# Global indices loaded first, a second column group for the global rows' values, fewer mask products, tile 0 in three pieces, and a new instruction order

## The chip, the cores and the metric

The kernel runs on one core of a Trainium2 chip (trn2). The metric is the device time of one execution in microseconds (us); lower is better.

## The reference

An attention with a window and a few global positions, followed by a two-layer network. Batch 8, 8 heads, 576 positions, 64 numbers a head, 8 global positions.

```python
scores = scale * np.matmul(q, k.transpose(0, 1, 3, 2))
mask = np.abs(pos[:, None] - pos[None, :]) <= 32
mask = mask | is_global[:, None] | is_global[None, :]
scores = np.where(mask, scores, -1e9)          # then softmax along the last axis
x = np.matmul(attn, v)                         # to (4608, 512): heads side by side
h = x @ w_in                                   # (4608, 2048)
g = np.maximum(h, 0.0) + np.log1p(np.exp(-np.abs(h)))   # softplus
out = g @ w_out                                # (4608, 512), float32
```

Only a band of the scores, the 8 global columns and the 8 global rows are computed.

## The kernel before

**The work's units.** Positions are cut into blocks of 32; a *pair* `n` is 4 blocks (128 tokens) of all 8 heads, so there are 36 pairs, 4.5 to a batch. Four pairs make a *tile* `m` of 512 tokens for the network; there are 9. A batch's keys and queries come in on SP's queue (L363, L413), are rounded to bf16 (`cast`, tiles `kb` and `qb`), and are turned (`turn`, L716 and L720) into `kx` and `qx`; its values become `vb`. There is one staging tile for each of q, k and v, so a batch's load can start when the batch before it has been rounded.

**A pair.** TensorE forms the scores `s` (L951). Pairs in `PARTED` (0 to 8) are masked on TensorE: two products of the mask with the identity (L935, L945) are put into the scores' banks first, VectorE takes the maxima (L966), and ACT takes eight exponentials with sums (L983). Other pairs are masked on VectorE: two adds (L955), the maxima (L968), a subtraction on GpSimd (L974), one exponential on ACT (L987), and the sums on VectorE (L994). GpSimd or VectorE divides (`pn`, L1002), VectorE transposes (`pt`, L1011), TensorE forms the values (`xo`, L1110), and ACT and VectorE copy them to `xT`.

**A batch's global rows.** The global queries against all keys (`sg`, L859), maxima (L869), exponentials (`pg`, L876), the transpose `pgt` (L881, L883), and the product with the values, `ov` (L892): 18 key blocks, four products of 32x32 weights and 129 columns each, all key blocks into the same place of one PSUM bank. `gv` (L897, L898) divides and gives `vg`, which `xo` needs.

**The network.** First layer `h` (L1140): 16 column blocks `c`, four products each; softplus on ACT (L1146) to `g`; second layer `o` (L1151): 16 products for each 128 tokens; ACT copies to `osb` and GpSimd or ACT stores. `HALVED = 2` lets tiles 0 and 1 go in two halves of 256 tokens.

**The order** is not written down. Each piece of work is a job with engines, planned costs, dependences, PSUM or buffer needs (`KINDS`, `SLOTS`: of the 8 banks `h` may hold 3) and a rank; `_Order.run` (L185) takes the job that can start first by its planned times, and each engine gets its instructions in that order and runs them strictly so. `stall` plans for TensorE's instruction fetch. `DRAWS` holds 39 random seeds that shift ranks and hold jobs back (`stir`). ACT's exponentials of the next tile are gated by the last softplus of the tile before (`gate`), and the rounding of batch b's keys and queries by the tenth softplus of tile b - 2.

Of the kernel before, what the change touches and what calls it, by code (L numbers as in the profile page):

```python
# [19 lines left out]
class _Order:  # L20
# [260 lines left out]
def kernel(  # L281
# [16 lines left out]
    P = 128  # L298
# [28 lines left out]
    PARTED = range(9)  # L327
    PIECES = 2
    HALVED = 2
    WARM = 34000  # L330
    DRAWS = (3335,3199,2819,96436,96805,4649,6481,3986,84270,10262,19837,43780,47955,95447,65550,91158,57715,12543,70958,16076,24438,75659,29538,93811,54424,2760,89415,85671,84841,4779,10200,27915,85360,19476,26792,78533,69364,53916,4150,)
# [253 lines left out]
    KINDS = dict(h=(3, 0), o=(2, 0), o0=(4, 0), s=(4, 0), tr=(3, 0), pick=(2, 0), sg=(4, 0), ov=(1, 0), xo=(4, 0))  # L585
# [94 lines left out]
    def add_cast(b, w):  # L680
# [6 lines left out]
        for h in range(2):  # L687
            def emit(e, h=h):
                if w == 2:
                    copy(e, vb[b % 2][:, :, h * D:(h + 1) * D], stage[2][:, h, :, :])  # L690
                else:
                    c = slice(h * 2 * NC, (h + 1) * 2 * NC)
                    (scaled, copy)[w](e, (qb, kb)[w][:, c, :, :].rearrange("p c d e -> p c e d"), stage[w][:, c, :, :])
            n = NJ * D
            cost = {"POOL": (1410, 1490), "ACT": (1380, 1480)}
            if b == 1:
                cost["DVE"] = (1290, 1370)
            if b == 0:
                cost = {"POOL": (1150, 1250), "DVE": (880, 960)}
            T["cast", b, w].append(o.add(cost, emit, [T["load", b, w]] + early + gate, rank=10 * phase_of(b) + 4 if b else 1.5 if w == 2 else 0))  # L700

    def add_prep(b):
# [97 lines left out]
        if early:  # L800
# [6 lines left out]
            for w, t in FIRST:  # L807
                for e in range(2 if t < FULL else 1):
# [6 lines left out]
                    T["last", w] = T["tr", b, w, t, e] = o.add({"PE": (330, 500) if b else (880, 1050) if t == 0 else (480, 650)}, lambda eng, w=w, t=t, e=e: tr(w, t, e),  # L815
# [18 lines left out]
        T["fill", b] = o.add({"DVE": (410, 490), "ACT": (470, 570)}, fill, [T["put", b, 1]] + blanked, rank=rank - 1 if b else 0, uses=[kkey])  # L834
# [11 lines left out]
    def add_global(b, gate):  # L846
# [39 lines left out]
        def ov(e, m0, m1):  # L886
            if m0 == 0:
                PS["ov", b] = psum(("ov", b), [P, 2 * D + 1], FP32)
            ps = PS["ov", b]
            for m in range(m0, m1):  # L890
                for c in range(R):
                    nc.tensor.matmul(out=ps[quad(c), :], lhsT=pgt[quad(c), m, 0:2 * NG, :].rearrange("p g h -> p (g h)"),  # L892
                                     rhs=vb[i][quad(c), m, 0:2 * D + 1], start=(m == 0), stop=(m == NJ - 1))
# [10 lines left out]
        heads = ((0, 1),) if b else ((0,), (1,))  # L904
        mxs, exps, tps, ovs = [], [], [], []
        for hs in heads:
            mxs.append(o.add({"DVE": (1680, 1760) if b else (860, 940)}, lambda e, hs=hs: mx(e, hs), [T["sg", b]], rank=rank, uses=keys, behind=mxs[-1:]))
        T["mxg", b] = mxs[-1]
        for xs in spans:
            for y, hs in enumerate(heads):  # L910
                exps.append(o.add({"ACT": (1780, 1880) if b else (430, 530)}, lambda e, xs=xs, hs=hs: gexp(e, xs, hs),
                                  [mxs[y], *gate, *free], rank=rank, uses=keys, table="exp", behind=exps[-1:]))
            m0, m1 = 2 * SPANS[xs[0]][0], 2 * sum(SPANS[xs[-1]])
            tps.append(o.add({"DVE": (990, 1070) if b else (540, 620)}, lambda e, m0=m0, m1=m1: tpg(e, m0, m1),
                             [*exps, T["make_own"]] + ([T["ov", b - 1]] if b else []), rank=rank - 1))
            ovs.append(o.add({"PE": (58 * (m1 - m0), 58 * (m1 - m0) + 170)}, lambda e, m0=m0, m1=m1: ov(e, m0, m1), [tps[-1], *ovs, *T["cast", b, 2]],
                             rank=3, array=32, ins=8 * (m1 - m0), opens=[] if ovs else [("ov", ("ov", b))], uses=[("ov", b)] if ovs else []))
        T["gexp", b], T["tpg", b], T["ov", b] = exps[-1], tps[-1], ovs[-1]
        T["gv", b] = o.add({"DVE": (400, 500)}, gv, [T["ov", b]] + [T["val", x] for x in old_vals(b - 2)],
                           rank=rank - 1, uses=[("ov", b)])  # L920

    def add_pair(n, gate):
# [106 lines left out]
        for y, (h0, h1) in enumerate(parts):  # L1029
# [15 lines left out]
            job = o.add({"POOL": (1040, 1040), "DVE": (620, 700)} if n < TP else pool(1905 * g // 8 + 90 * (g < 8)), lambda e, y=y: no(e, y), [job], rank=at,  # L1045
# [10 lines left out]
    for m in range(NT):  # L1056
        VALS += [(m, [m * TP, m * TP + 1]), (m, [m * TP + 2, m * TP + 3])] if m < HALVED else [(m, list(range(m * TP, (m + 1) * TP)))]
# [8 lines left out]
    def add_values(v_):  # L1066
# [46 lines left out]
        def xev(e, r):  # L1113
            copy(e, PS["xT", m][:, r, part * cols:(part + 1) * cols], PS["xo", v_, r][:, 0:cols])
# [19 lines left out]
    def add_moe(m, exps):  # L1134
        nt = TT

        def first(e, c, key, lo, hi):
            h = PS[key] = psum(key, [P, hi - lo], FP32)
# [4 lines left out]
        def soft(e, c, key, lo, hi):  # L1143
            if lo == 0:
                PS["g", m, c] = gp.tile([P, nt], BF16, tag=f"g{c}", name=f"g{c}")
            nc.scalar.activation(out=PS["g", m, c][:, lo:hi], in_=PS[key][:, :], func=AF.Softplus)  # L1146

        def second(e, ns, kf):
            if kf == 0:
                PS["o", m, ns] = psum(("o", m, ns), [P, d_model], FP32)  # L1150
            nc.tensor.matmul(out=PS["o", m, ns][:, :], lhsT=PS["g", m, kf][:, ns * P:(ns + 1) * P],  # L1151
                             rhs=w_out_t[kf // 4][:, kf % 4, :], start=(kf == 0), stop=(kf == KF - 1))

        def oev(e, ns):
            t = PS["osb", m, ns] = op.tile([P, d_model], FP32, tag="osb", name="osb")
            copy(e, t[:, :], PS["o", m, ns][:, :])
            if m >= OWN:
                store(nc.scalar, ns)

        def store(eng, ns):  # L1160
            n0 = m * TT + ns * P
            eng.dma_start(out=out[n0:n0 + P, :], in_=PS["osb", m, ns][:, :])  # L1162
        vs = [x for x in range(len(VALS)) if VALS[x][0] == m]
        cuts = [(i * nt // len(vs), (i + 1) * nt // len(vs)) for i in range(len(vs))]
        own = []
        for i, (lo, hi) in enumerate(cuts):
            x_ready = [T["xev", vs[i], r] for r in range(KD)]
            own.append({})
            for c in range(KF):
                key = ("h", m, c, i)  # L1170
                T["first", m, c] = o.add(mm(KD, hi - lo), lambda e, c=c, k=key, a=lo, z=hi: first(e, c, k, a, z),
                                         x_ready + [T["w_in", c // 4]], rank=5, ins=2 * KD, opens=[("h", key)], uses=[("xT", m)])
                T["soft", m, c] = o.add({"ACT": (500, 600) if hi - lo > 256 else (270, 370)},
                                        lambda e, c=c, k=key, a=lo, z=hi: soft(e, c, k, a, z), [T["first", m, c], *exps], rank=10 * m + 2,
                                        opens=[] if i else [(f"g{c}", ("g", m, c))],
                                        uses=[key] + ([("g", m, c)] if i else []), table="soft", behind=[own[0]["soft", c]] if i else [])
                own[i]["soft", c] = T["soft", m, c]
            own[i]["first"] = T["first", m, KF - 1]
        for ns in range(nt // P):
            last = None  # L1180
            mine = own[ns * len(cuts) * P // nt]
            for kf in range(KF):
                last = o.add(mm(1, d_model), lambda e, ns=ns, kf=kf: second(e, ns, kf),
                             [mine["soft", kf], T["w_out", kf // 4], last, mine["first"] if m < NT - 1 else None],
                             rank=6,
                             opens=[("o" if m else "o0", ("o", m, ns))] if kf == 0 else [], uses=[("g", m, kf), ("o", m, ns)])
            T["second", m, ns] = last
            T["oev", m, ns] = o.add({"ACT": (600, 700)} if m < OWN else {"ACT": (950, 700)}, lambda e, ns=ns: oev(e, ns), [last], rank=3,
                                    opens=[("osb", ("osb", m, ns))], uses=[("o", m, ns)])
            if m < OWN:  # L1190
                o.add({"POOL": (700, 2700)}, lambda e, ns=ns: store(nc.gpsimd, ns), [T["oev", m, ns]], rank=-0.5, hold=2000,
# [125 lines left out]
```

## Time and profile before

| | us |
|---|---|
| median of 3 runs | 347.17 |
| the runs | 344.98, 347.17, 352.44 |
| the profiled execution: time | 347.77 |
| its span | 346.1 |
| TensorE busy | 321.8 (93%) |
| ACT busy | 239.7 (69%) |
| VectorE busy | 213.3 (62%) |
| GpSimd busy | 180.8 (52%) |

The span runs from the first to the last instruction. In rows of the profile, PE is TensorE, PEld its weight loads, DVE VectorE, ACT ScalarE, POOL GpSimd and SP SyncE; SPq is SP's DMA queue. A row by groups has line, engine, operation, output and inputs, shapes and count, then busy us and mean ns of one, then the idle us before them and what ended it. A row of the timeline or the chain of waits has start, us, and what ran.

### The profile page before, as it was taken

The numbers are of one execution on the slowest core, as the hardware profiler recorded it, in microseconds if no ns is written. First come the engines' busy times: TensorE is split into PE (matmuls) and PEld (weight loads), VectorE is DVE, ScalarE is ACT, GpSimd is POOL, SyncE is SP. The second block draws the span as 40 slices with busy tenths as digits, with TensorE's granted clock in tenths as the row PEclk, the third lists the DMA queues.
The fourth block names the chain that finished last, engine by engine and source line by source line (L and its number), as shares of the span: only waits on it lengthen the run. The fifth ranks groups of instructions, "written<-read, shape, count | busy, mean of one in ns | idle before, by whom it ended". The sixth has DMA issues, their size and how long they took to land.

```text
span 346.1 us, 12041 instructions
## 1 busy us (share of the span) xinstructions
PE 321.8 (93%) x5186; PEld 173.0 (50%) x5233; DVE 213.3 (62%) x381; ACT 239.7 (69%) x506; POOL 180.8 (52%) x166
## 2 busy tenths in 40 slices
PE   6849999989998999799999999999999989999995
PEld 2625884457655445444464445444644444445442
DVE  6898721976989939862999479927980870071000
ACT  4689889897894788267919792979277846746531
POOL 5756504592989685883579338934771460060000
PEclk9667999999999999999999999999999999999999
DMA  6999799989999899971998892710100010011011
GB/s 186 213 185 257 139 185 194 200 168 184 161 191 202 148 185 171 204 148 25 165 179 170 133 161 78 156 45 2 64 32 30 35 61 2 30 72 54 0 49 74
DMA packets 168589, 42.74 MB, mean 123 GB/s; under 512 B 153176, under 2 KB 165464, under 8 KB 168536
## 3 DMA queue, kind: packets, MB, share of 16 engines
q1 hardware_dynamic: 160664, 28.33, 46.5%
q0 software_dynamic: 6144, 10.49, 13.1%
q10 hardware_dynamic: 1728, 3.15, 2.4%
q8 instruction: 41, 0.67, 0.8%
q14 instruction: 12, 0.10, 0.1%
HBM read 36.71 MB, written 9.44 MB: 133 GB/s over the span
## 4 chain that ended last, share of the span: by engine, by line
PE 57%; SPq 14%; DMA 8%; DVE 8%; ACT 4%; issue 4%; POOL 3%; DVEq 0%; POOLq 0%; ACTq 0%
PE h L1140 24%; PE o L1151 22%; SPq L363 10%; SPq L368 4%; PE xo L1110 3%; PE ov L892 3%; DMA wout<-in_moe_w_out_dram 2%; DMA stage<-in_k_dram 2%; DMA stage<-in_q_dram 2%; PE s L951 2%; POOL pn L1002 1%; DMA stage<-in_v_dram 1%; DVE gm L869 1%; DVE pgt L881 1%; DVE sm L994 1%
## 5 line engine op out<-in xcount | busy, mean ns | idle before, releaser
L1140 PE MATMUL h<-xT,win 128*128 128x512 bf16 (+1 forms) x691 | 132.1, 340 | 2.2 <-issue 1.3
L1151 PE MATMUL o<-wout,g 128*128 128x512 bf16 x545 | 128.7, 379 | 4.1 <-issue 3.3
L1002 POOL TENSOR_TENSOR pn<-st,rs 128x1024 bf16<-128x1024 f32 (+1 forms) x43 | 67.5, 1580 | 87.1 <-ACT osb L621 41.3
L1146 ACT ACTIVATE g<-h 128x512 bf16<-128x512 f32 (+1 forms) x176 | 86.2, 526 | 30.3 <-PE h L1140 24.0
L1140 PEld LDWEIGHTS <-win 128*128 128x128 bf16 x704 | 67.1, 98 | 58.0 <-issue 2.5
L1151 PEld LDWEIGHTS <-g 128*128 128x128 bf16 x576 | 53.6, 98 | 63.6 <-issue 1.4
L974 POOL TENSOR_TENSOR st<-st,m 128x1024 f32<-128x1024 f32 x27 | 51.0, 1897 | 15.8 <-DVE m L968 15.7
L994 DVE TENSOR_REDUCE sm<-st 128x8 f32<-128x1024 f32 x27 | 32.2, 1194 | 22.3 <-ACT st L987 22.2
L621 ACT COPY osb<-o 128x512 f32<-128x512 f32 x36 | 21.6, 600 | 32.8 <-PE o L1151 27.8
L955 DVE TENSOR_TENSOR st<-s,mask 128x512 f32<-128x512 f32 x54 | 34.4, 674 | 1.9 <-PE s L951 1.9
L968 DVE TENSOR_REDUCE m<-st 128x8 f32<-128x1024 f32 x27 | 32.4, 1207 | 0.3
L987 ACT ACTIVATE st<-st 128x1024 f32<-128x1024 f32 x27 | 27.6, 1063 | 0.5 <-ACT osb L621 0.4
L1011 DVE STREAM_TRANSPOSE pt<-pn 128x512 int32<-128x512 int32 x36 | 25.0, 694 | 3.9 <-POOL pn L1002 3.8
L983 ACT ACTIVATE st<-s,m 128x128 f32<-128x128 f32 x72 | 25.4, 420 | 1.3 <-DVE rs L996 1.1
L621 ACT CAST xT<-xo 128x512 bf16<-128x512 f32 (+1 forms) x19 | 9.5, 557 | 21.1 <-PE xo L1110 21.1
L869 DVE TENSOR_REDUCE gm<-sg 128x1 f32<-128x320 f32 (+1 forms) x32 | 12.4, 446 | 18.8 <-PE sg L859 18.8
L1162 POOL DMA_DIRECT2D out_dram<-osb x24 | 13.9, 581 | 11.9 <-ACT osb L621 11.9
L983 ACT ACTIVATION_READ_ACCUMULATOR st<-s,m 128x1 f32 x72 | 18.6, 260 | 0.0
L720 DVE STREAM_TRANSPOSE kx<-kb 128x1152 int32<-128x1152 int32 x6 | 8.2, 1360 | 14.4 <-ACT kb L621 10.8
L621 DVE CAST xT<-xo 128x256 bf16<-128x256 f32 (+1 forms) x25 | 12.7, 543 | 7.0 <-PE xo L1110 6.9
L951 PEld LDWEIGHTS <-qx 64*32 64x32 bf16 x1152 | 10.1, 93 | 13.4 <-issue 11.6
L876 ACT ACTIVATE pg<-sg,gnb 128x320 bf16<-128x320 f32 (+1 forms) x32 | 15.1, 578 | 2.3 <-DVE gnb L870 1.7
(120 smaller groups left out, 319.2 us busy)
## 6 DMA issues: line engine op xcount, KB each, us to landing
stage<-in_v_dram SPq DMA_DIRECT2D x64, 144.0 KB, 4.3
stage<-in_k_dram SPq DMA_DIRECT2D x48, 144.0 KB, 4.0
stage<-in_q_dram SPq DMA_DIRECT2D x48, 144.0 KB, 3.9
out_dram<-osb POOLq DMA_DIRECT2D x24, 256.0 KB, 3.3
out_dram<-osb ACTq DMA_DIRECT2D x12, 256.0 KB, 2.3
stage<-in_q_dram SPq DMA_DIRECT2D x4, 512.0 KB, 4.3
stage<-in_k_dram SPq DMA_DIRECT2D x4, 512.0 KB, 8.3
win<-in_moe_w_in_dram POOLq DMA_DIRECT2D x4, 512.0 KB, 8.6
```

What stands on the lines that cost most here:

```text
L363: eng.dma_start(out=stage[w][quad(r), :, e, :], in_=SRC[w][b, HG * g:HG * g + HG].rearrange("a (c i e) (f d) -> e f i (a c) d", i=BL, e=2, ...
L621: {"ACT": nc.scalar.copy, "DVE": V.tensor_copy, "POOL": nc.gpsimd.tensor_copy}[e](out, in_)
L955: V.tensor_tensor(out=PS["st", n][:, h, :, :], in0=PS["s", n, h][:, :, :], in1=mask[:, h, j0:j0 + PB, :, :].rearrange("p j s i -> p j (s i ...
L968: V.reduce_max(out=m[:], in_=flat(PS["st", n], h0, h1), axis=AX)
L974: nc.gpsimd.tensor_tensor(out=t, in0=t, in1=over(PS["m", n, y][:], SL * BL), op=OP.subtract)
L983: nc.scalar.activation(out=t[:, x, :], in_=PS["s", n, h0][:, x, :], func=AF.Exp, bias=PS["m", n, y][:, x:x + 1], accum_out=sm[:, x:x + 1])
L987: nc.scalar.activation(out=t, in_=t, func=AF.Exp)
L994: V.reduce_sum(out=sm[:], in_=flat(PS["st", n], h0, h1), axis=AX)
L1002: on(e).tensor_tensor(out=PS["pn", n][:, :, :, h0:h1].rearrange("p x s h -> p h x s"), in0=PS["st", n][:, h0:h1], in1=PS["rs", n, y][:].re ...
L1140: nc.tensor.matmul(out=h[:, :], lhsT=w_in_t[c // 4][:, kd, c % 4 * P:(c % 4 + 1) * P], rhs=PS["xT", m][:, kd, lo:hi], start=(kd == 0), sto ...
L1146: nc.scalar.activation(out=PS["g", m, c][:, lo:hi], in_=PS[key][:, :], func=AF.Softplus)
L1151: nc.tensor.matmul(out=PS["o", m, ns][:, :], lhsT=PS["g", m, kf][:, ns * P:(ns + 1) * P], rhs=w_out_t[kf // 4][:, kf % 4, :], start=(kf == ...
```

## The change

- `global_idx` is loaded ahead of the first queries on SP's queue.
- `ov`: even key blocks stay; odd ones go to the column group two further on and to a second bank. Two 64-row copies (`odd`, by ACT or VectorE) and an add put the halves together before `gv`. `KINDS` gives `ov` two banks.
- `PARTED` is 4: pairs 4 to 8 are masked on VectorE.
- Tile 0 goes in pieces of 1, 2 and 1 pairs (`PIECED`), 128, 256 and 128 columns; several column blocks share a bank, and softplus waits for the bank's last.
- In batch 0 the two head groups' maxima are one job.
- The last 128 tokens' second layer, copy and store go in two halves of 256 columns.
- Some planned costs, the planned fetch time (`FETCH`, `SLOW`) and the seeds change, and with them the order on every engine. SP's order changes in the indices only. Of the rounding, batch 4's two query halves move from GpSimd to ACT; on ACT they and one key half stand between softplus operations of tile 2: ten softplus, `qb`, two, `kb`, three, `qb`, one.

```diff
-    FETCH = 3700
+    FETCH = 3900
+    SLOW = (170000, 4600, 3600)
...
-                last = max(here, last) + self.FETCH
+                until, early, later = self.SLOW
+                last = max(here + (early if here < until else later), last + self.FETCH)
...
-    PARTED = range(9)
+    PARTED = range(4)
     PIECES = 2
-    HALVED = 2
+    PIECED = {0: (1, 2, 1), 1: (2, 2)}
...
+    nc.sync.dma_start(out=gi[:, :], in_=global_idx.rearrange("(one n) -> one n", one=1).bitcast(I32)
+                      .to_broadcast([P, 2 * NG]))
     for w, t in FIRST:
         load_part(0, w, t)
-        if (w, t) == FIRST[0]:
-            nc.sync.dma_start(out=gi[:, :], in_=global_idx.rearrange("(one n) -> one n", one=1).bitcast(I32)
-                              .to_broadcast([P, 2 * NG]))
...
-    KINDS = dict(h=(3, 0), o=(2, 0), o0=(4, 0), s=(4, 0), tr=(3, 0), pick=(2, 0), sg=(4, 0), ov=(1, 0), xo=(4, 0))
+    KINDS = dict(h=(3, 0), o=(2, 0), o0=(4, 0), s=(4, 0), tr=(3, 0), pick=(2, 0), sg=(4, 0), ov=(2, 0), xo=(4, 0))
...
             for m in range(m0, m1):
                 for c in range(R):
-                    nc.tensor.matmul(out=ps[quad(c), :], lhsT=pgt[quad(c), m, 0:2 * NG, :].rearrange("p g h -> p (g h)"),
-                                     rhs=vb[i][quad(c), m, 0:2 * D + 1], start=(m == 0), stop=(m == NJ - 1))
+                    nc.tensor.matmul(out=PS["ov", b, m % 2][quad(c ^ 2 * (m % 2)), :], lhsT=pgt[quad(c), m, 0:2 * NG, :].rearrange("p g h -> p (g h)"),
+                                     rhs=vb[i][quad(c), m, 0:2 * D + 1], start=(m < 2), stop=(m >= NJ - 2))
+
+        def odd(e):
+            t = PS["odd", b] = sb.tile([P, 2 * D + 1], FP32, tag="odd", name="odd")
+            for x in range(2):
+                copy(e, t[rows(x), :], PS["ov", b, 1][rows(1 - x), :])
 
         def gv(e):
             rs = sb.tile([P, 1], FP32, tag="grs", name="grs")
-            V.reciprocal(rs[:], PS["ov", b][:, 2 * D:2 * D + 1])
-            V.tensor_scalar(out=vg[i][:], in0=PS["ov", b][:, 0:2 * D], scalar1=rs[:, 0:1], scalar2=None, op0=OP.mult)
+            both = PS["odd", b]
+            V.tensor_tensor(out=both[:], in0=PS["ov", b, 0][:, :], in1=both[:], op=OP.add)
+            V.reciprocal(rs[:], both[:, 2 * D:2 * D + 1])
+            V.tensor_scalar(out=vg[i][:], in0=both[:, 0:2 * D], scalar1=rs[:, 0:1], scalar2=None, op0=OP.mult)
...
         def first(e, c, key, lo, hi):
-            h = PS[key] = psum(key, [P, hi - lo], FP32)
+            if lo_of(c, hi - lo) == 0:
+                PS[key] = psum(key, [P, 512 // (hi - lo), hi - lo], FP32)
+            h = PS[key][:, lo_of(c, hi - lo)]
...
+            sides = [(0, d_model)] if (m, ns) != (NT - 1, TP - 1) else [(0, d_model // 2), (d_model // 2, d_model)]
```

More of the change, by code (lines that the diff above doesn't have):

```diff
@@ L903, in add_global @@
         spans = ((0, 1),) if b else ((0,), (1,))
-        heads = ((0, 1),) if b else ((0,), (1,))
+        heads = ((0, 1),)
         mxs, exps, tps, ovs = [], [], [], []
         for hs in heads:
-            mxs.append(o.add({"DVE": (1680, 1760) if b else (860, 940)}, lambda e, hs=hs: mx(e, hs), [T["sg", b]], rank=rank, uses=keys, behind=mxs[-1:]))
+            mxs.append(o.add({"DVE": (1700, 1780)}, lambda e, hs=hs: mx(e, hs), [T["sg", b]], rank=rank, uses=keys, behind=mxs[-1:]))
         T["mxg", b] = mxs[-1]
@@ L1056 @@
     for m in range(NT):
-        VALS += [(m, [m * TP, m * TP + 1]), (m, [m * TP + 2, m * TP + 3])] if m < HALVED else [(m, list(range(m * TP, (m + 1) * TP)))]
+        n0 = m * TP
+        for n in PIECED.get(m, (TP,)):
+            VALS.append((m, list(range(n0, n0 + n))))
+            n0 += n
     def old_vals(b):
@@ L1180, in add_moe @@
             last = None
[L1181 to L1189, printed above, removed]
+            mine = next(x for x, (lo, hi) in zip(own, cuts) if lo <= ns * P < hi)
+            sides = [(0, d_model)] if (m, ns) != (NT - 1, TP - 1) else [(0, d_model // 2), (d_model // 2, d_model)]
+            for a, z in sides:
+                for kf in range(KF):
+                    last = o.add(mm(1, z - a), lambda e, ns=ns, kf=kf, a=a, z=z: second(e, ns, kf, a, z),
+                                 [mine["soft", kf], T["w_out", kf // 4], last, mine["first"] if m < NT - 1 else None]
+                                 + (had(*[("second", m, n) for n in range(ns)]) if a else []), rank=6,
+                                 opens=[("o" if m else "o0", ("o", m, ns, a))] if kf == 0 else [], uses=[("g", m, kf), ("o", m, ns, a)])
+                T["second", m, ns] = last
+                T["oev", m, ns] = o.add({"ACT": (600, 700)} if m < OWN else {"ACT": (950, 700)}, lambda e, ns=ns, a=a, z=z: oev(e, ns, a, z), [last], rank=3,
+                                        opens=[("osb", ("osb", m, ns))] if a == 0 else [], uses=[("o", m, ns, a)] + ([("osb", m, ns)] if a else []))
             if m < OWN:
-                o.add({"POOL": (700, 2700)}, lambda e, ns=ns: store(nc.gpsimd, ns), [T["oev", m, ns]], rank=-0.5, hold=2000,
+                o.add({"POOL": (700, 2700)}, lambda e, ns=ns: store(nc.gpsimd, ns, 0, d_model), [T["oev", m, ns]], rank=-0.5, hold=2000,
                       uses=[("osb", m, ns)])
```

78 lines of the change are left out of this document (43 added, 35 removed).

## The prediction, made before the changed kernel ran

> **What bounds the kernel now.** First the page's busy times, then the busy time by stretch, over six stretches that I chose where the page's slices change.
>
> ```profile
> span 346.1 us, 12041 instructions
> PE 321.8 (93%) x5186; PEld 173.0 (50%) x5233; DVE 213.3 (62%) x381; ACT 239.7 (69%) x506; POOL 180.8 (52%) x166
> ...
> 0.00:30.00 30.00, 20.68 (x391) 11.84 (x393) 23.46 (x65) 20.93 (x76) 17.98 (x40) 0.72 1.05 199
> 30.00:60.00 30.00, 29.73 (x481) 21.68 (x473) 13.64 (x34) 26.63 (x88) 12.12 (x21) 1.00 1.05 190
> 60.00:80.00 20.00, 17.53 (x444) 10.68 (x446) 15.02 (x37) 17.80 (x69) 14.20 (x15) 1.00 0.97 192
> 80.00:120.00 40.00, 38.36 (x828) 23.39 (x836) 36.35 (x53) 30.27 (x56) 29.43 (x20) 1.00 0.96 172
> 120.00:200.00 80.00, 76.46 (x1285) 38.20 (x1296) 56.62 (x86) 55.22 (x86) 52.31 (x36) 1.00 0.84 152
> 200.00:342.40 142.40, 139.00 (x1799) 67.25 (x1802) 68.23 (x108) 88.26 (x135) 54.71 (x37) 1.00 0.21 55
> ```
>
> The columns are PE, its weight loads, DVE, ACT, POOL, granted clock, DMA share, GB/s. From 30 to 342.4 us TensorE is busy 301.1 of 312.4 us at full clock, so a microsecond less of its work is a microsecond less of time, unless its next work is late. The second bound stands in the DMA column: to 120 us the 16 DMA engines are full. After 200 us they have room. So two questions decide: how much TensorE work goes, and whether inputs keep up until the loads have run ahead. The execution took 347.77 us, 1.67 around its span.
>
> **Masks of pairs 4 to 8.** Five pairs lose their two mask products; the mask is added on VectorE, as for later pairs.
>
> ```profile
> 61.23 0.59 PE L945 MATMUL s<-mask,ident 128*128 128x512 bf16 x2
> 61.75 0.42 PE L951 MATMUL s<-kx,qx 64*32 64x128 bf16 x32
> 62.10 1.47 PE L1151 MATMUL o<-wout,g 128*128 128x512 bf16 x6
> ```
>
> From start to start the two products take 0.52 and the scores 0.35. Five times 0.52 is 2.6 us of TensorE. In exchange VectorE gets, per pair:
>
> ```profile
> L955 DVE TENSOR_TENSOR st<-s,mask 128x512 f32<-128x512 f32 x54 | 34.4, 674 | 1.9 <-PE s L951 1.9
> L968 DVE TENSOR_REDUCE m<-st 128x8 f32<-128x1024 f32 x27 | 32.4, 1207 | 0.3
> L994 DVE TENSOR_REDUCE sm<-st 128x8 f32<-128x1024 f32 x27 | 32.2, 1194 | 22.3 <-ACT st L987 22.2
> L966 DVE TENSOR_REDUCE m<-s 128x4 f32<-128x512 f32 x18 | 11.6, 676 | 1.7 <-PE s L951 1.7
> ```
>
> That is 1.35 + 1.21 + 1.19 in place of 1.35: 2.4 more, 12 us for five. VectorE has 16.4 us free between 30 and 60 us, so I cost it at nothing; without that cover it is the second rival below. POOL's added subtraction and ACT's fewer exponentials lie in the same free stretch.
>
> **Odd key blocks on another column group (ov).** Eight batches, 72 products each. No row shows the new form; the nearest are products that alternate between column groups already, scores and values:
>
> ```profile
> 172.57 0.69 PE s L951 x64
> 173.26 1.16 PE ov L892 x72
> ...
> 213.63 1.56 PE xo L1110 x147
> ```
>
> That is 16 ns a product for ov, 10.8 and 10.6 for the others. At 10.8, 72 take 0.78: a gain of 0.38 each, 2.7 us for the seven batches at full clock. Bounds: nothing, and 0.58 with half the time gone (0 to 4.1 us in all). I take 0.38, since both neighbours agree. Speaking against it, the Trainium skill's "TensorE: Matmul & The Clock Gate" (section "Wait — 56ns, not 53.3ns?") says that products never start closer than about 25 ns; by it ov would gain nothing. The 16 ns above already lie below that, so the trace disagrees for products on separate parts of the array.
> The evacuation becomes two copies, an add and a second bank. The copies wait for ov on ACT (on VectorE in two batches), with the store's copies and the next exponentials queued behind them; 11 to 22 output products (0.216 each, so 2.4 us and more) stand between ov and the values in the new order from batch 1 on, which hides this. Without them it would cost what the two copies and the add take, some 1 us a batch by the 0.37 of a 256-column copy (row further down).
>
> **Tile 0 in pieces, indices first, the end.**
>
> ```profile
> 6.48 0.17 DVE L484 CAST gf<-gi 128x8 f32<-128x8 int32 x1 [1.90 <-DMA gi<-in_global_idx_dram]
> 15.78 1.34 ACT L621 COPY qx<-tr 128x512 bf16<-128x512 bf16 x2 [1.56 <-PE tr L747]
> 35.49 0.40 PE L747 MATMUL tr<-ident,qb 128*128 128x128 bf16 x4
> 35.72 0.24 PE L753 MATMUL pick<-hot,qb 128*128 128x8 bf16 x4
> 44.03 8.47 PE L1140 MATMUL h<-xT,win 128*128 128x256 bf16 x76
> ```
>
> 128 columns cost (35.72 - 35.49)/4 = 0.058, 256 cost 8.47/76 = 0.111. Two pieces of 128 and one of 256 instead of two of 256: 64 x (2 x 0.058 - 0.111) = 0.3 us more. The indices move ahead of the first queries on SP's queue, which are asked for 0.5 us later (bounds for that: 0 and 0.5). The wait of 1.90 goes, but the keys, which come no sooner, then hold the scores up. What reaches the path is that VectorE takes one of the two query copies (half of 1.34) from ACT ahead of the exponentials. I take 0.7 us off the start, bounds 0 and 1.9. The last output block in two halves: the last copy of 0.58 becomes one of 256 columns:
>
> ```profile
> L621 ACT CAST xT<-xo 128x256 bf16<-128x256 f32 x3 | 1.0, 374 | 1.3 <-PE xo L1110 1.3
> 342.46 0.58 ACT L621 COPY osb<-o 128x512 f32<-128x512 f32 x1 [2.87 <-PE o L1151]
> ```
>
> I take 0.3 with its smaller store, bounds 0 and 0.6.
>
> If nothing else held: 2.6 + 2.7 + 0.7 + 0.3 - 0.3 = 6.0 us less.
>
> **What the new order waits for.** The loads of batches 2 to 5 follow each other on SP without a break. Here are batch 4's keys and queries on SP, the chain of waits from their landing on, and TensorE and ACT at that time:
>
> ```profile
> 102.75 11.26 SPq L363 DMA_DIRECT2D stage<-in_k_dram  x8
> 114.10 8.84 SPq L363 DMA_DIRECT2D stage<-in_q_dram  x8
> ...
> 122.23 3.35 DMA stage<-in_q_dram
> 126.17 2.91 POOL qb L618 x2
> 129.10 1.38 DVE qx L716
> ...
> 135.77 1.23 PE ov L892 x72
> ...
> 117.29 10.53 PE L1140 MATMUL h<-xT,win 128*128 128x512 bf16 x47
> ...
> 122.69 0.60 ACT L1146 ACTIVATE g<-h 128x512 bf16<-128x512 f32 x1 [0.27 <-PE h L1140]
> 124.04 1.48 ACT L621 CAST kb<-stage 128x1152 bf16<-128x1152 f32 x1
> ...
> L614 ACT ACTIVATE qb<-stage 128x1152 bf16<-128x1152 f32 x3 | 4.6, 1539 | 0.0
> ```
>
> They land at 125.6 and GpSimd, with nothing urgent behind it, rounds both halves. In the new order ACT rounds both, amid tile 2's softplus: ten softplus, a half, two softplus, a key half, three softplus, the other half, the last softplus. The tenth softplus (row of 122.69) ends at 123.3 now, and earlier with TensorE ahead; the loads, bound by full DMA engines with the same packets and the same start, are not. So ACT stands until 125.6, casts until 127.1, and the eleventh softplus ends at 127.7. TensorE's first-layer products may hold three banks, so it stops after 13 of 16 column blocks and ends the last three (12 x 0.216) at 130.4, where it now ends at 127.7 (117.29 + 10.53, less the overlap to the next row). The 3.8 us that it had won to here (2.6 + 2 x 0.38 + 0.7 - 0.3) turn into waiting, and it is 2.7 behind. The second half is rounded at 127.7 + 0.5 + 1.5 + 1.6 + 1.5 = 132.8, so batch 4's query transpose starts 3.7 us later than at 129.10, and on VectorE the maxima of batch 3's global rows stand behind it, for whose values ov waits.
>
> What is left then, against now: one score pair less (0.35), five ov (5 x 0.38 = 1.9), the end (0.3), the second-layer split 0.1 more. Two instruction waits I take as gone, because the new order breaks up the runs before them: 14 output products now stand between batch 4's picks and its scores, and 22 ahead of the values:
>
> ```profile
> 139.83 0.36 PE L951 MATMUL s<-kx,qx 64*32 64x128 bf16 x24 [1.11 <-issue]
> 144.11 0.73 PE L1110 MATMUL xo<-pt,vb 32*64 32x96 bf16 x67 [0.46 <-issue]
> ```
>
> Bounds for this: 3 us won or lost. Sum: 2.7 - 0.35 - 1.9 - 0.3 + 0.1 - 1.5 = -1.25; span 344.9, profiled execution 346.5. The profiled execution lies 0.6 above the median of the three runs, so 345.9.
>
> **The rivals.**
> First, the queries don't hold ACT up, because they land some 4 us sooner or the softplus gets there later. Then the 6.0 us stay, with the 1.5 us of instruction waits: 347.77 - 7.5 - 0.6 = 339.7. For it: 8.84 us for eight transfers is slow beside 6.86 for the batch before (row below), so neighbours' stores may have slowed them; against it: full engines and equal bytes.
>
> ```profile
> 89.66 6.86 SPq L363 DMA_DIRECT2D stage<-in_q_dram  x8
> ```
>
> Second, VectorE: if its 12 us more up to 80 us don't fit into the free time, tile 2 comes late. Decisive is whether batch 1's ov waits for its transposed probabilities by over 5 us. Up to 4 us of it vanish in the wait for batch 4's queries; with 9 of 12 us uncovered, 5 remain: 350.9, slower.
> Third, the clock. The stop at 124 us lasts about 3.7 us.
>
> ```profile
> 22.00:24.00 2.00, 0.15 (x8) 0.15 (x12) 1.97 (x5) 2.00 (x8) 0.83 (x1) 0.50 1.18 172
> 29.00:30.00 1.00, 1.00 (x57) 0.65 (x57) 0.69 (x3) 1.00 (x7) 0.82 (x1) 0.68 1.16 311
> ```
>
> After an idle stretch at 22 us the clock was 0.50 and came back only in the second from 29. Six microseconds at half speed cost 3: 348.9. It decides if the idle passes some 3 us. The Trainium skill's "TensorE: Matmul & The Clock Gate" (section "What's actually happening") puts the fall at one idle window of about 3.4 us; the rows agree that the clock halves, and nothing here fixes the 3.4.
> Fourth, ov doesn't quicken: 1.9 us back, 347.8.
>
> **How the numbers follow.** Forecast 0.42, own range 341 to 350; the first rival 0.38, the second 0.07, the third 0.07, the fourth 0.02; 0.04 for waits that I haven't followed, in batches 5 to 7. A difference under 2%, 6.9 us, is about what a measurement of this kernel can tell from none: faster means under 340.2, slower over 354.1. Two thirds of the first rival (0.26) and 0.05 of the forecast, with all its bounds on the good side, are faster: 0.31. Half of the second and third rivals, where 3 us of new waits come on top, and the 0.04 are slower: 0.11. The rest is 0.58. The range runs from 338, below the first rival, to 353, above the second with 2 us of waits.
>
> **What would show it.** No mask products outside four pairs; ov near 0.8 us; ACT idle before a query cast in the middle of tile 2's softplus, released by the queries' transfer near 125 us; TensorE idle 3 to 4 us there; tile 2's first layer ending near 130. Wrong if ACT doesn't wait there and values of tile 3 start before 143, or if ov stays at 1.2.

## The result and the profile after

The changed kernel took 355.62 us (355.42 to 355.85, 4 runs) beside 346.90 of the kernel before: a ratio of 1.0261, 95% interval 1.0219 to 1.0303, slower. On two chips of the experiments below it took 351.79 (1.0131, 1.0099 to 1.0164) and 353.45 (1.0213, 1.0163 to 1.0262). The forecast was 345.9, range 338 to 353. The profiled execution took 355.85, with a span of 354.1.

First the page's busy times and its chain of waits, with the chain of before under it, then the stretches that the prediction showed of before.

```profile
span 354.1 us, 12267 instructions
PE 323.5 (91%) x5327; PEld 171.8 (49%) x5327; DVE 238.9 (67%) x397; ACT 235.8 (67%) x463; POOL 188.5 (53%) x167
PE 51%; DVE 25%; SPq 10%; ACT 6%; DMA 4%; issue 3%; DVEq 0%; ACTq 0%
```

```profile
PE 57%; SPq 14%; DMA 8%; DVE 8%; ACT 4%; issue 4%; POOL 3%; DVEq 0%; POOLq 0%; ACTq 0%
```

```profile
0.00:30.00 30.00, 18.95 (x340) 9.40 (x341) 22.23 (x64) 19.32 (x70) 16.92 (x39) 0.74 1.11 206
30.00:60.00 30.00, 24.35 (x618) 19.12 (x617) 22.27 (x49) 18.93 (x67) 16.75 (x22) 0.92 1.00 188
60.00:80.00 20.00, 18.86 (x328) 10.57 (x326) 16.80 (x28) 17.03 (x33) 13.33 (x10) 1.00 0.99 181
80.00:120.00 40.00, 38.04 (x770) 23.84 (x761) 31.17 (x45) 30.96 (x64) 26.77 (x21) 1.00 0.94 168
120.00:200.00 80.00, 75.62 (x1304) 36.81 (x1303) 65.38 (x94) 52.44 (x81) 56.00 (x39) 1.00 0.73 141
200.00:350.40 150.40, 147.03 (x1988) 71.70 (x1986) 81.03 (x120) 96.73 (x152) 58.77 (x39) 1.00 0.23 59
```

Three things stand out. VectorE has 238.9 us of work where it had 213.3: 25.6 more, and the prediction had worked out 12 for the masks. VectorE now makes a quarter of the chain that ends last; before it was 8%. And TensorE does 43.3 us of work in the first 60 (18.95 + 24.35), where it did 50.4.

The masks' own operations did grow by about 12 us. Where VectorE's other 13 come from is in the groups, first those of before, then those of after (the last figure ahead of the second bar is the mean ns of one, behind that bar stands idle time):

```profile
L898 DVE TENSOR_SCALAR vg<-ov,grs 128x128 bf16<-128x128 f32 x8 | 2.8, 351 | 0.3
L883 DVE COPY pgt<-own 128x288 bf16<-128x288 bf16 x7 | 3.4, 489 | 0.2
L892 PE MATMUL ov<-vb,pgt 32*32 32x129 bf16 x576 | 10.8, 227 | 3.9 <-DVE pgt L883 3.6
```

```profile
L906 DVE TENSOR_SCALAR vg<-odd,grs 128x128 bf16<-128x128 f32 x8 | 10.4, 1301 | 0.3
L884 DVE COPY pgt<-own 128x288 bf16<-128x288 bf16 x7 | 10.3, 1478 | 0.2
L893 PE MATMUL ov<-vb,pgt 32*32 32x129 bf16 x576 | 7.0, 230 | 11.0 <-DVE pgt L884 11.0
```

The scaling to `vg` does the same work on the same shape and takes 3.7 times as long: 7.6 us more. The only difference is its input: `ov` in PSUM before, the tile `odd` in SBUF now. The copy of the own rows behind the transpose `pgt` isn't touched by the diff and takes 6.9 us more. The two together, 14.5, are a little more than the 13 looked for; smaller changes make up the difference. `ov` itself became quick, 7.0 us of work for 10.8, and TensorE waits 11.0 us in front of it, where it waited 3.9: 6.28 of the 11.0 in batch 0, which is told further down, and 4.7 in the later batches.

Now VectorE, then GpSimd, around batch 3's `ov`:

```profile
142.34 2.10 DVE L884 COPY pgt<-own 128x288 bf16<-128x288 bf16 x1
144.37 0.70 DVE L1020 STREAM_TRANSPOSE pt<-pn 128x512 int32<-128x512 int32 x1
...
146.32 0.25 DVE L904 TENSOR_TENSOR odd<-ov,odd 128x129 f32<-128x129 f32 x1
146.61 0.16 DVE L905 RECIPROCAL grs<-odd 128x1 f32<-128x1 f32 x1
146.81 1.74 DVE L906 TENSOR_SCALAR vg<-odd,grs 128x128 bf16<-128x128 f32 x1
```

```profile
141.83 0.58 POOL L1180 DMA_DIRECT2D out_dram<-osb  x1
142.44 1.91 POOL L1011 TENSOR_TENSOR pn<-st,rs 128x1024 bf16<-128x1024 f32 x1
146.57 1.90 POOL L1011 TENSOR_TENSOR pn<-st,rs 128x1024 bf16<-128x1024 f32 x1 [2.23 <-DVE odd L904]
```

The copy ends at 144.44 and GpSimd's product at 144.35; the scaling at 148.55 and GpSimd's next product at 148.47. Both VectorE operations end 0.1 us after the GpSimd product that runs beside them. In this trace so do all seven 128x288 copies and seven of the eight scalings; the eighth, batch 0's, has no GpSimd operation beside it and takes 0.29. The same stretch on TensorE:

```profile
144.50 0.80 PE L893 MATMUL ov<-vb,pgt 32*32 32x129 bf16 x72 [1.49 <-DVE pgt L884]
145.24 4.92 PE L1168 MATMUL o<-wout,g 128*128 128x512 bf16 x22
150.09 0.29 PE L1122 MATMUL xo<-pt,vg 32*64 32x192 bf16 x8
...
151.74 0.35 PE L1122 MATMUL xo<-pt,vg 32*64 32x320 bf16 x8 [0.88 <-DVE pt L1020]
```

TensorE waits 1.49 for the copy, and 0.88 for a transpose of VectorE (151.02 to 151.68) that stands behind the long scaling. The kernel before has the counterexample: its scaling, from PSUM, takes 0.35 in the middle of GpSimd's 99.65 to 102.56, and its copy starts 0.11 before GpSimd's product ends (97.50 + 1.90 = 99.40), in time for the gap until 99.65. GpSimd first, then VectorE:

```profile
97.50 1.90 POOL L1002 TENSOR_TENSOR pn<-st,rs 128x1024 bf16<-128x1024 f32 x1 [1.40 <-DVE rs L996]
99.65 2.91 POOL L618 TENSOR_SCALAR qb<-stage 128x1152 bf16<-128x1152 f32 x2 [0.25 <-issue]
```

```profile
99.29 0.23 DVE L883 COPY pgt<-own 128x288 bf16<-128x288 bf16 x1
101.55 0.35 DVE L898 TENSOR_SCALAR vg<-ov,grs 128x128 bf16<-128x128 f32 x1
```

### The profile page after: what moved, and what is told of

Read it like the earlier page. It is cut to its first block, busy times and chain, and to the rows that moved or that the text cites. A ratio compares the mean times of both kernels' runs of the same rounds, so it can differ in the third digit from the quotient of the medians.

```text
span 354.1 us, 12267 instructions
## 1 busy us (share of the span) xinstructions
PE 323.5 (91%) x5327; PEld 171.8 (49%) x5327; DVE 238.9 (67%) x397; ACT 235.8 (67%) x463; POOL 188.5 (53%) x167
## 4 chain that ended last, share of the span: by engine, by line
PE 51%; DVE 25%; SPq 10%; ACT 6%; DMA 4%; issue 3%; DVEq 0%; ACTq 0%
PE h L1157 30%; PE o L1168 13%; DVE sm L1003 7%; SPq L365 5%; DVE pt L1020 4%; PE xo L1122 4%; DMA stage<-in_v_dram 4%; SPq L370 3%; DVE pgt L884 3%; DVE vg L906 3%; PE s L960 2%; ACT st L996 2%; DVE gm L870 1%; DVE pgt L882 1%; ACT g L1163 1%
## 5 line engine op out<-in xcount | busy, mean ns | idle before, releaser
L1168 PE MATMUL o<-wout,g 128*128 128x512 bf16 (+1 forms) x592 | 134.0, 374 | 0.0
L1157 PE MATMUL h<-xT,win 128*128 128x512 bf16 (+2 forms) x768 | 133.8, 328 | 0.0
L1163 ACT ACTIVATE g<-h 128x512 bf16<-128x512 f32 (+2 forms) x192 | 86.0, 499 | 33.5 <-PE h L1157 30.3
L983 POOL TENSOR_TENSOR st<-st,m 128x1024 f32<-128x1024 f32 x32 | 60.3, 1894 | 29.4 <-DVE m L977 29.4
L1003 DVE TENSOR_REDUCE sm<-st 128x8 f32<-128x1024 f32 x32 | 38.0, 1188 | 18.3 <-ACT st L996 18.1
L622 ACT COPY osb<-o 128x512 f32<-128x512 f32 (+1 forms) x37 | 21.1, 572 | 28.3 <-PE o L1168 22.8
L977 DVE TENSOR_REDUCE m<-st 128x8 f32<-128x1024 f32 x32 | 38.3, 1207 | 0.2
L622 ACT CAST xT<-xo 128x512 bf16<-128x512 f32 (+2 forms) x25 | 11.8, 528 | 22.2 <-PE xo L1122 22.1
L717 DVE STREAM_TRANSPOSE qx<-qb 128x1152 int32<-128x1152 int32 x6 | 8.2, 1370 | 16.8 <-ACT qb L615 13.6
L960 PE MATMUL s<-kx,qx 64*32 64x128 bf16 x1152 | 15.5, 227 | 2.7 <-issue 2.7
L893 PE MATMUL ov<-vb,pgt 32*32 32x129 bf16 x576 | 7.0, 230 | 11.0 <-DVE pgt L884 11.0
L1122 PE MATMUL xo<-pt,vb 32*64 32x96 bf16 (+2 forms) x1328 | 14.5, 211 | 0.9 <-issue 0.9
```

The source lines that it names most:

```text
L622: {"ACT": nc.scalar.copy, "DVE": V.tensor_copy, "POOL": nc.gpsimd.tensor_copy}[e](out, in_)
L960: nc.tensor.matmul(out=PS["s", n, g][quad(a ^ g), x, :], lhsT=qx[b % 2][rows(g), a, j * BL:(j + 1) * BL], rhs=kx[b % 2][rows(g), a, e0 * B ...
L977: V.reduce_max(out=m[:], in_=flat(PS["st", n], h0, h1), axis=AX)
L983: nc.gpsimd.tensor_tensor(out=t, in0=t, in1=over(PS["m", n, y][:], SL * BL), op=OP.subtract)
L1003: V.reduce_sum(out=sm[:], in_=flat(PS["st", n], h0, h1), axis=AX)
L1157: nc.tensor.matmul(out=h[:, :], lhsT=w_in_t[c // 4][:, kd, c % 4 * P:(c % 4 + 1) * P], rhs=PS["xT", m][:, kd, lo:hi], start=(kd == 0), sto ...
```

## The experiments

An order can be held: the list of pieces of work, with their engines, is taken from one kernel and given to the planner of another, so that every engine's row stays as it was except for pieces that are new. In four of the kernels with a held order (the first and the third below, and both that have `ov` in the order of before) the planner's filler products (`warm`) are capped as well; their traces have 19 to 21 of them, the kernel before 21.

```diff
     o.stir(DRAWS)
+    o.given = [...]    # pieces of work and engines, from the other kernel
```

**Is it the opening or the later order?** Two kernels with all of the change but the opening's order and tile 0's pieces exchanged, and one with three parts of the change in the order of before.

> The changed kernel, but every engine's row up to the planned 50 us stands as in the kernel before (tile 0 in two pieces, batch 0's global maxima by halves), and as in the changed kernel from there on. Theory A, the 8 us are lost in the opening, before 64 us: TensorE is busy some 54 us of the first 64 again instead of 47.3, and the time falls by 7 to 10 us from 355.6, to 346 to 349. Theory B, VectorE is late in the new order after 64 us (TensorE's waits on VectorE 10.7 us there): the opening gives 2 us at most and the time stays at 353 to 356.

> The changed kernel, with every engine's row up to the planned 50 us as in the changed kernel, and from there on as in the kernel before. Theory A: the opening's loss stays and the later work loses nothing new; 346.9 + 9 for the opening, less about 4 for masks and ov later: 350 to 353. Theory B: with the old order after 50 us the waits on VectorE shrink from 10.7 us to under 4, and the time falls to 343 to 347.

> The kernel before in its own order, with three parts of the change put in: indices first, ov on two column groups, masks of pairs 4 to 8 on VectorE. By the sum of the prediction 2.6 + 2.7 + up to 0.7 us go: 341 to 342. If VectorE's 12 us more and the copies behind ov come late instead (the rival), 346 to 349, with TensorE waiting on VectorE for over 4 us.

Measured: 369.4 (ratio to before 1.0642, 1.0579 to 1.0705), 366.7 (1.0530, 1.0434 to 1.0626) and 369.1 (1.0652, 1.0595 to 1.0708). None of the theories gave that; the test failed as a test of A against B. It shows something else, here in the third kernel on TensorE:

```profile
64.16 1.46 PE L1161 MATMUL o<-wout,g 128*128 128x512 bf16 x6 [0.16 <-issue]
72.37 1.18 PE L894 MATMUL ov<-vb,pgt 32*32 32x129 bf16 x72 [6.76 <-DVE pgt L885]
```

With the masks of pairs 4 to 8 on VectorE in an order made for other lengths, batch 1's `ov` waits 6.76 us: the row that the second rival named. VectorE isn't short of time there: it stands idle for 10.54 us until 59.30 and for 3.25 us until 70.68. The new work comes at the wrong places of its row. So these three parts don't fit the order of before, and the new order isn't an extra of the change; that no small rearrangement would do isn't shown.

**Single parts.** The changed kernel with the indices second again; the kernel before with `ov` and the last block's halves alone; the kernel before with the indices first alone.

```diff
     for w, t in FIRST:
         load_part(0, w, t)
+        if (w, t) == FIRST[0]:
+            nc.sync.dma_start(out=gi[:, :], ...)    # taken out ahead of the loop
```

> The changed kernel with the indices asked for second again, nothing else. If asking for them first is what makes batch 0's values land late (23.5 us instead of before 21.8), the first ov starts 1 to 2 us sooner than at 25.62 and the time is 353 to 355. If it isn't, the keys only come 0.5 us later and the time is 355.5 to 356.5.

> The kernel before in its own order, with two parts of the change: ov on two column groups with its two copies and the add, and the last output block in halves. If the sum of the prediction holds (7 x 0.38 and 0.3): 343.5, with ov's 72 products in 0.75 to 0.80 us and no new wait of over 1 us. If the copies and the add behind ov come late for the values in an order that leaves them no room: 346 to 349, with TensorE waiting for the global values or ACT's copies in most batches.

> The kernel before in its own order, with the indices asked for first and nothing else. The prediction had 0 to 1.9 us less. If the new place of that small transfer makes batch 0's values land late by itself: VectorE or GpSimd wait for them past 21.8 us and the time is 347.5 to 350. If it only does so with the changed kernel's start: 345.5 to 347.

Measured: 352.73 (1.0164, 1.0108 to 1.0219), 353.17 (1.0210, 1.0158 to 1.0263) and 348.19 (1.0021, 0.9979 to 1.0064). The indices alone change nothing that can be measured, and as that kernel's order is held too, holding an order costs nothing by itself. `ov` costs 6 us in the old order, though its 72 products take 0.80 there too (1.02 in one batch): the other outcome, and more than the 346 to 349 given for it. The first result, 2.9 us below the changed kernel's first measurement, came from another chip; side by side it did not come back:

> The changed kernel itself, beside the next one on one chip: 355 to 356 as measured before.

> The changed kernel with the indices asked for second, as before (352.7). If that order costs the changed kernel something, 2 to 3.5 us less than the run of the changed kernel beside it; if the first comparison only caught another chip or state, within 1 us of it.

Measured on one chip: 351.79 (1.0131, 1.0099 to 1.0164), not the 355 to 356 expected, and 353.42 (1.0190, 1.0150 to 1.0231). The 2.9 us were not the indices' place.

**Is it VectorE?**

```diff
-                V.reduce_sum(out=sm[:], in_=flat(PS["st", n], h0, h1), axis=AX)
+                V.reduce_sum(out=sm[:], in_=flat(PS["st", n], h0, h1)[:, :, BL:3 * BL], axis=AX)
```

> The changed kernel in its own order; the sums of the exponentials of the 32 unmasked pairs run over 64 of 128 columns, so part of each sum is left out, and VectorE gets some 0.55 us less per pair, 18 us in all. If the later loss is VectorE's lateness in front of ov and the values (10.7 us of waits after 64 us), these waits fall below 6 us and the time falls by 3 to 6 us, to 350 to 352.5. If VectorE is only named there and something else ends the waits (GpSimd's subtractions and products, ACT), the time stays within 1 us of 355.6.

Measured: 344.62 (0.9954, 0.9925 to 0.9984), a larger fall than the first theory's 350 to 352.5. VectorE's lateness is what the end waits for, but this kernel doesn't tell work from waiting: the scaling's median there is still 1340 ns.

**Does the first stop on TensorE come from the weights' transfer?** On GpSimd, two of the four requests for the second layer's weights go behind the first subtraction.

> The changed kernel with the indices second (352.7 before this) and, on GpSimd, the third and fourth request for the second layer's weights one subtraction later (at some 48 us instead of 38). If TensorE's 2.4 us stop at 42.7 to 45.1, put down to nothing that the profile shows, is its next instructions arriving late behind those weights on the DMA engines, it shrinks under 1 us and the time is 350 to 351.5. If it is only the number of small products in a row, it stays at 2 to 2.7 us and the time at 352 to 354 (over that where the weights then come late for the second layer).

Measured: 356.06 (1.0268, 1.0194 to 1.0343). Nothing is won; without this edit the kernel had taken 352.73 and 353.42 on other chips. The stop itself comes and goes: it was 2.37 us, until 45.11, in the first trace of the kernel with the indices second, and in the second trace of the same kernel the scores at 44.96 start without one. So a single run can't tell what removes it, and what causes it stays open.

**The scaling's source.** The deciding edit is two lines. The sum stays in PSUM; the work, the order and the number of instructions stay.

```diff
-            V.tensor_tensor(out=both[:], in0=PS["ov", b, 0][:, :], in1=both[:], op=OP.add)
+            V.tensor_tensor(out=PS["ov", b, 0][:, :], in0=PS["ov", b, 0][:, :], in1=both[:], op=OP.add)
+            both = PS["ov", b, 0]
```

> The changed kernel in its own order; the add behind ov writes its sum over ov's own bank in PSUM instead of into SBUF, so that the scaling to vg reads PSUM again as it did before the change. Theory C: the scaling grew from 0.35 us to a median of 1.45 because its operands now all lie in SBUF and it stands still until GpSimd's running operation ends (146.81 + 1.74 = 148.55, GpSimd 146.57 + 1.90 = 148.47). Then it takes 0.35 again, and the time falls by 0.9 us for each batch whose values wait: 349 to 353. Theory D, VectorE simply has too much work and the scaling's length is an effect of being late: it stays above 1 us and the time at 355 to 356.

> The changed kernel itself, beside the next one: 351.8 if batch 0's values land before 21 us (as in the run with that time), 355.6 if at 23.5 us (as in the first).

> The changed kernel with the add's sum in PSUM. Theory C: the seven later scalings take 0.95 us less each, so 4 to 6 us below the run of the changed kernel beside it; the rest of the first comparison's 8 us was the opening on another chip. If the scaling was worth all 8, 7 to 9 below.

Measured: 347.30 (1.0024, 0.9986 to 1.0062) on one chip; on another, side by side, 353.45 for the changed kernel and 346.45 (1.0005, 0.9974 to 1.0037) with the sum in PSUM. That is 7.0 us less, nearly the 7.6 by which the eight scalings had grown; 4 to 6 had been expected, or 7 to 9 if it were worth all.

```profile
L907 DVE TENSOR_SCALAR vg<-ov,grs 128x128 bf16<-128x128 f32 x8 | 2.8, 351 | 0.3
```

Theory C holds and theory D falls: the work and the order are otherwise the same, and the operation is short again wherever it stands. TensorE's waits for the copy stay, 4.7 us after 64 us.

Three more kernels with this edit: with the copy of the own rows left out as well, with the indices second, and `ov` in the order of before.

```diff
+            if b == 0:
                 V.tensor_copy(pgt[:, m0:m1, NG:2 * NG, :]..., own[:, m0:m1]...)
```

> As the kernel before this one, and the copy of the batch's own rows into the transposed probabilities is left out for batches 1 to 7 (that part of the computation is missing): 235 ns in the kernel before, 1434 in the changed one. By theory C the copy, too, waits for GpSimd (142.34 + 2.10 = 144.44, GpSimd 142.44 + 1.91 = 144.35), and TensorE's waits of ov for it (4.7 us after 64 us) nearly vanish: another 3 to 6 us, 344 to 349. By theory D: 1 us at most.

> The changed kernel with the add's sum in PSUM and the indices asked for second. If the two losses are separate (indices 2.9 us, scaling some 3): 347 to 350, about the kernel before. If they fall into the same waits: no better than the better one of the two.

> The kernel before in its own order, with ov on two column groups and the last block in halves (353.2 so), and the add's sum in PSUM. By theory C the scaling takes 0.35 us and what ov wins reaches the end: 343 to 346.5. By theory D, or if the copies on ACT and the add are what comes late: 350 to 353.

Measured: 343.06 (0.9896, 0.9857 to 0.9936), 348.41 (1.0039, 0.9994 to 1.0083) and 349.82 (1.0094, 1.0058 to 1.0130). The copy is worth 4.2 us beside 347.30, measured on the same chip. The indices give nothing. `ov` in the old order wins some 3.4 of its 6 us back (two chips) and is still slower than before, while theory C had given 343 to 346.5. VectorE stands idle there for 6.0 us in front of its eight adds, waiting for ACT's copies `odd`, which the prediction took as hidden in the new order; how much of these 6.0 reaches the end isn't shown.

**The copy without its wait, and both repairs.** VectorE's reductions kept their length in both kernels, with GpSimd at work beside them (the maxima 1207 ns on average before and after, the sums 1194 and 1188). A maximum over an axis of length one copies.

```diff
-            V.tensor_copy(pgt[:, m0:m1, NG:2 * NG, :].rearrange("p m g h -> p m (g h)"),
-                          own[:, m0:m1].rearrange("p m g h -> p m (g h)"))
+            V.reduce_max(out=pgt[:, m0:m1, NG:2 * NG, :].rearrange("p m g h -> p m (g h)"),
+                         in_=own[:, m0:m1].rearrange("p m g h -> p m (g h)").unsqueeze(3), axis=AX)
```

> The changed kernel in its own order; the copy of the own rows is done as a maximum over an axis of length one, which gives the same values. Theory C: reductions of VectorE kept their 1.19 to 1.21 us beside a working GpSimd in both kernels, so this one takes 0.3 to 0.5 us instead of a median of 1.43 and the time falls by 3 to 5 us, to 350.5 to 352.5, though the scaling still waits. Theory D: any operation there is long, because VectorE is late: over 1 us, and 355 to 356.

> Both repairs, the whole computation: the add's sum in PSUM and the copy as a maximum. Theory C: 343.5 to 345.5, near the 343.1 of the kernel that leaves the copy out, and below the kernel before (346.6). If the maximum costs what the copy's wait did: 347.

Measured, on the chip where the changed kernel took 351.79: 347.50 (0.9993, 0.9965 to 1.0021) and 342.74 (0.9879, 0.9832 to 0.9926). The whole computation with both repairs beats the kernel before by 1.2% and the changed one by 9 us. Around batch 3's `ov`, in the kernel with both:

```profile
140.05 0.45 DVE L884 TENSOR_REDUCE pgt<-own 128x288 bf16<-128x288 bf16 x1
...
143.08 0.35 DVE L907 TENSOR_SCALAR vg<-ov,grs 128x128 bf16<-128x128 f32 x1
```

```profile
139.56 1.91 POOL L1012 TENSOR_TENSOR pn<-st,rs 128x1024 bf16<-128x1024 f32 x1
142.63 1.90 POOL L1012 TENSOR_TENSOR pn<-st,rs 128x1024 bf16<-128x1024 f32 x1 [1.16 <-ACT odd L622]
```

```profile
141.09 0.80 PE L893 MATMUL ov<-vb,pgt 32*32 32x129 bf16 x72
141.82 4.92 PE L1169 MATMUL o<-wout,g 128*128 128x512 bf16 x22
...
147.24 0.39 PE L1123 MATMUL xo<-pt,vg 32*64 32x320 bf16 x8
```

GpSimd's products again run beside both VectorE operations, both run through, and TensorE waits neither in front of `ov` nor in front of the values. After 64 us TensorE waits 1.7 us for VectorE in this kernel, where it waits 10.7 in the changed one.

## Why the prediction was wrong, point by point

**The step that failed** is the costing of `ov`'s evacuation at nothing, as hidden by "11 to 22 output products". It counted the two copies and the add, the pieces that the diff adds, and let the scaling stand at its old length without a word. The add moved the scaling's input into SBUF, and with that a scaling ends only when GpSimd's product beside it does: 0.35 became 1.30 on average, 7.6 us more in eight, and putting the sum back into PSUM takes 7.0 us off the time. The rows that could have told were in the trace of before: the 128x288 copy `pgt<-own`, with both sides in SBUF, took between 0.23 and 1.03 us there, while the scaling from PSUM always took 0.35. Here are both of batch 5, and GpSimd's products beside them:

```profile
205.25 1.03 DVE L883 COPY pgt<-own 128x288 bf16<-128x288 bf16 x1
...
207.82 0.35 DVE L898 TENSOR_SCALAR vg<-ov,grs 128x128 bf16<-128x128 f32 x1
```

```profile
204.30 1.89 POOL L1002 TENSOR_TENSOR pn<-st,rs 128x1024 bf16<-128x1024 f32 x1 [4.17 <-DVE rs L996]
...
207.80 1.89 POOL L1002 TENSOR_TENSOR pn<-st,rs 128x1024 bf16<-128x1024 f32 x1 [1.08 <-DVE grs L897]
```

The copy ends at 206.28, 0.1 after GpSimd's 206.19; the scaling runs through inside GpSimd's product. The Trainium skill's "SBUF — State Buffer" (section "Who interferes with whom") states the rule: VectorE's copies, casts and scalings can take a mode that holds the port pair shared with GpSimd, whoever comes second blocks until the other is done, and on this chip reductions never do so. The skill's "VectorE: DVE Perf Modes" (section "What auto-detection actually checks") ties that mode to a source and a destination in SBUF. The traces agree on the operations: ends within 0.1 us of GpSimd's, 0.35 from PSUM, 0.45 for the reduction. On who comes second they are less plain: the copy of 142.34 starts 0.1 us before the product that it ends with, while GpSimd is still at a store (141.83 + 0.58 = 142.41), and so does the scaling of 253.74, by 0.2. It is the rule against this change that the prediction should have weighed and didn't.

**A second miss: the copy.** The order was read for what it moves on TensorE and ACT, not for which VectorE copies now stand beside GpSimd. Doing it as a reduction gives 4.3 us (351.79 to 347.50). The two repairs overlap: 7.0 and 4.3 singly, 9.05 together.

**The sizes of the gains were about right.** Mask products stand for pairs 0 to 3 alone, and `ov` takes 0.74 us from start to start, against 0.78. "If nothing else held" gave 6.0 us less; with the two waits taken away the change gives 4.6 (347.34 to 342.74). What each part gives of that is not measured singly.

**The start: wrong.** The prediction took 0.7 us off. The first scores come 1.2 us earlier (12.84 for 14.04), but in the first profile batch 0's values landed late, VectorE stood idle for 3.26 us in front of its cast of them, and TensorE behind it. VectorE's row, TensorE's rows, and the stretch 48 to 52 of the changed kernel:

```profile
23.55 0.76 DVE L622 CAST vb<-stage 128x1152 bf16<-128x1152 f32 x1 [3.26 <-DMA stage<-in_v_dram]
```

```profile
25.62 0.74 PE L893 MATMUL ov<-vb,pgt 32*32 32x129 bf16 x40 [6.28 <-DVE pgt L884]
47.81 0.31 PE L960 MATMUL s<-kx,qx 64*32 64x128 bf16 x16 [2.66 <-issue]
```

```profile
48.00:52.00 4.00, 4.00 (x77) 2.81 (x61) 2.41 (x3) 2.07 (x5) 1.90 (x1) 0.57 1.24 219
```

Then TensorE stopped 2.66 us in its scores for nothing that the profile shows, and had little more than half the clock for the next microseconds (0.57 is the granted clock). In a later run, on a chip where the time was 351.79, the values landed in time and the same `ov` began at 22.45 and waited 3.90; batch 1's `ov` began at 67.25 for 70.98, and that execution was 3.4 us shorter. So the opening's loss varies from run to run, and between these two executions it makes up the whole difference. The landing alone doesn't set it: with the sum in PSUM, an execution whose values landed at 23.42 took 348.27, and one whose values landed by 19.96 took 348.00. What decides when the values land isn't settled.

**Batch 4's queries: the landing right, the consequence wrong.** The changed kernel is so late by then that ACT doesn't wait at all. In the kernel with both repairs it does; ACT's row, then TensorE's:

```profile
125.69 1.52 ACT L615 ACTIVATE qb<-stage 128x1152 bf16<-128x1152 f32 x1 [4.37 <-DMA stage<-in_v_dram]
```

```profile
120.91 5.35 PE L1158 MATMUL h<-xT,win 128*128 128x512 bf16 x24
129.52 0.47 PE L777 MATMUL pick<-kb,pick 128*32 128x128 bf16 x18 [1.53 <-ACT kb L622]
132.29 0.46 PE L777 MATMUL pick<-qb,pick 128*32 128x128 bf16 x18 [2.30 <-ACT qb L615]
```

ACT stands 4.37 us until 125.69; forecast was 125.6. (The row names the values' transfer. Releasers are inferred, and SP asks for the first of the values only at 122.74, right behind the last of the queries, so I read it as the queries' landing.) But TensorE's last 24 first-layer products run through, six column blocks ahead of the softplus. The limit of three banks is the planner's, by its own times; it doesn't hold TensorE back there. The price came later, 1.53 + 2.30 us ahead of batch 4's picks, in place of 3.7 in the middle of the layer.

**Instruction waits.** Taken as gone around 140 and 144 us, and gone: none of the longer ones is left after 64 us. Two new ones, 2.66 and 0.94, stand in the opening. TensorE's waits after 64 us in the changed kernel (sum, how many, longest):

```profile
PE ov L893 <- DVE pgt L884: 4.7, 6, 1.5
PE xo L1122 <- DVE st L964: 3.1, 4, 1.3
PE xo L1122 <- DVE pt L1020: 2.3, 4, 0.9
PE xo L1122 <- DVE vg L906: 0.6, 1, 0.6
```

Together 10.7 us, all for VectorE.

**The rivals.** The second named the right engine, with too little room for its work, at the wrong place: batch 1's `ov` waits 0.2 us in the changed kernel, and the loss comes in most batches, from operations that stand still rather than from 12 us of masks. The third, the clock, showed in the opening and not at 124 us: 0.92 over 30 to 60 us costs at most 30 x 0.08 = 2.4 us. The fourth is ruled out by `ov`'s 0.80. The first, 339.7, is what the change comes near to once its new waits are gone (342.7), but not for the first rival's reason: there the queries do hold ACT up.

## What to carry to other kernels

Cost not only the operations that an edit adds, but also those whose operands it moves: an add that lands in SBUF instead of PSUM made the untouched operation behind it 3.7 times as long. Look in the trace of before for operations of one shape whose shortest and longest times lie far apart; find what ends the long ones (here GpSimd's product), for a new order that puts more of them beside it pays each time. And when parts of a change are tested alone in an order held from another kernel, the misfit of the order itself can cost more than the part.

## What the runs showed of the hardware

- A VectorE scaling of 128x128 from SBUF to SBUF took 0.29 us alone and up to 2.20 beside GpSimd; from PSUM 0.35 always. A 128x288 copy of bf16 in SBUF: 0.23 alone, up to 2.10 beside GpSimd in the changed kernel; as a maximum over one element 0.45 always. VectorE's transposes to `pt` (694 and 688 ns on average, before and after), its reductions of 1024 columns (1.19 to 1.21 us) and its adds of the mask with one operand in PSUM (674 and 675 ns) kept their lengths.
- `ov` on two column groups: 72 products of 32x32 weights and 129 columns in 0.80 us, 0.74 from start to start, some 10.3 to 11.1 ns a product (1.23 and 1.16 us, 16 ns, on one).
- The same instructions, with the same transfers asked for at the same places, had batch 0's values landed by 19.6 us in one run and at 23.55 in another.
